# Row transposes of the second to fifth expert: two blocks (three tiles, then two) in place of five groups of four

## The chip, the cores and the metric

The kernel runs on one core of one Trainium2 chip. The metric is the device time of one execution in microseconds (us). Three executions of the kernel before took 602.71, 602.74 and 603.37 us, median 602.74.

## The reference

Two stages. The first is a causal decayed attention without softmax: for 8 batches and 8 heads of 576 positions by 64 dimensions, `scores = q k^T / 8`, multiplied by a decay matrix `gamma_h ** (i - j)` for `i >= j` (zero above the diagonal), times `v`. Its output is rearranged to 4608 rows (tokens) of 512.

The second is a mixture of eight experts with a fixed capacity. `logits = x @ w_gate` (4608 x 8); all 36,864 pairs of token and expert are sorted by logit, and in that order a token goes to the expert if it has none yet and the expert has fewer than 576 tokens. Each expert then has exactly 576 rows, and its output is `relu(x[mask] @ w1[e]) @ w2[e]`, with w1 of 512 x 1024 and w2 of 1024 x 512, written back to the rows' places.

## The kernel before, in words

The attention takes the first quarter of the time. What follows is the routing and the experts, interleaved: while TensorE multiplies for one expert, VectorE finds by a radix search which 576 tokens go to a later expert. The eight experts are handled in the order in which the search fills them; below they are called the first to the eighth (`e` = 0 to 7 in the code).

Every float32 operand is split into a high and a low part (`xh`, `xl`; `w1h`, `w1l`; ...), and a product is three matmuls (high by high, low by high, high by low). For one expert the work runs like this:

- `gather(e)` (line 1061): POOL issues five indirect DMAs (L1072) that bring the 576 rows of the expert into the tile `xg`, 128 rows each, the last one 64. It also sets `state['arrives']`, the planner's time from which the rows are taken to be there.
- `transposes(e)` (line 1127), a generator: for each of the five row tiles j, four TensorE transposes (L1163) of 128 x 128 into one PSUM tile `pt`; then ScalarE copies it to `xh` (L1165), and VectorE makes `xl` (L1166). The five tiles `pt` lie in PSUM under the tags t, h0, h1, h0, h1. The tag t has one buffer, h0 and h1 have two each, taken in turn. The first expert uses the tags t and y instead, and experts from the sixth on are transposed in other ways (lines 1136 and 1129).
- `l1(e, tr)` (line 1172): 16 tiles `ph` (8 blocks of hidden units x 2 parts of the rows, 256 and 320), 12 matmuls each (L1209). Their PSUM buffers are of the same tags h0 (first part) and h1 (second part), but for the third and the sixth pair, which use y. ScalarE writes the high part after the ReLU (L1219), and `low` on VectorE the low part (L1181: one instruction for a 256-row tile, two for a 320-row one). `low` of a tile is issued one tile later; that of the sixteenth and last is kept in `owed` and issued in the next stage.
- `l2(e, hb)` (line 1337): five row tiles t of 8 steps f each (L1357): three matmuls of 512 columns in a step, two for the last row tile. In each step, after the matmuls: `mix.adv` (the planner), `owed` at f = 1 (line 1360), gathers, weight conversions (`conv`, L1000 and L1010 on ScalarE, L1012 on POOL), and then lines 1373 to 1375: when the planner's time has passed `state['arrives']`, the generator of the next expert's transposes is made, and from then on one `next(tr)` is called per step. So each group of four transposes comes behind one step's matmuls.

The order on each engine is fixed when the program is built, by a planner (`Mixer`, line 885). It keeps a time `t` for TensorE (each step adds its estimate, 650 ns in `l2`, 430 for the last row tile) and `v` for VectorE (`mix.vec(610)` for each transposed tile, for example). A step of the search (nine matmuls L357 on TensorE, then about 15 VectorE instructions, L361 to L352) is put in at the first `mix.adv` at which `t` has passed the time that `v` allows; some of them (line 354, third entry) one `adv` later. Engines execute in that order; what is computed from what is guarded by semaphores. `pt` in a buffer that a `ph` held before waits until that tile's ScalarE and VectorE readers are done.

The lines that write, read and hold the buffers: line 1161 takes the PSUM tile of a group, line 1202 that of an `l1` tile:

```
pt = P['bank'](("t", "h0", "h1", "h0", "h1")[j] if e else ("t", "y", "y", "t", "y")[j], [128, 4, 128], "pt", F32R)
ps = P['bank']("y" if i // 2 in (2, 5) else f"h{s}", [128, n], "ph")
```

Of the kernel before, what the change touches and what calls it, by code (L numbers as in the profile page):

```python
# [11 lines left out]
F32 = mybir.dt.float32  # L12
F32R = mybir.dt.float32r
# [3 lines left out]
ALU = mybir.AluOpType  # L17
AF = mybir.ActivationFunctionType
# [921 lines left out]
def moe(tc, nc, P, R, xd, w1_d, w1q_d, w2_d, out, mix):  # L940
    V, A, T = nc.vector, nc.scalar, nc.tensor
# [4 lines left out]
    state = dict(dma=0, conv=0, most=2, listing=-1, force=False, asked=set())  # L946
# [114 lines left out]
    def gather(e, all=False, behind=None):  # L1061
        if e == E or not ready(e):
            return
        if e not in state['asked']:
            state['asked'].add(e)
            if e not in XG:
                XG[e] = P["c"].tile([128, 20, 128], F32, name="xg", tag="xg")
            xg = XG[e]
            if e < QUART:
                for j in range(5):  # L1070
                    n = 128 if j < 4 else 64
                    nc.gpsimd.indirect_dma_start(out=xg[:n, 4*j:4*j+4, :].rearrange("p a c -> p (a c)"), out_offset=None, in_=xd[:, :],  # L1072
                                                 in_offset=bass.IndirectOffsetOnAxis(ap=found[e][:n, j:j+1], axis=0))
                state['arrives'] = mix.t + (11800 if e == 3 else 9000)
            else:
                LEFT[e] = list(range(18))
                state['arrives'], state['next'], state['at'] = 0, 0, {}
        left = LEFT.get(e)
        while left and (all or mix.t >= state['next']):
            g = left.pop(0)  # L1080
            if behind is not None:
                nc.gpsimd.tensor_copy(spacer4, behind.bitcast(F32))
            nc.gpsimd.indirect_dma_start(out=XG[e][:, g, :], out_offset=None, in_=xq,  # L1083
                                         in_offset=bass.IndirectOffsetOnAxis(ap=lines[e][:, g:g+1], axis=0))
            state['next'] = mix.t + 1200
            state['at'][g] = mix.t + (6000 if e >= FAST else 13000)

    def fast_transposes(e):

        xg = XG[e]  # L1090
        x = P['s'].tile([128, 4, 2, 288], F32, name="xt", bufs=1)
        xh, xl = [P['s'].tile([128, 7, 2, 288], F32R, name=n, bufs=1) for n in ("xh", "xl")]
        XH[e], XL[e] = xh, xl
        high = lambda i, q: A.activation(xh[:, i], x[:, q], AF.Copy)
        low = lambda i, q: V.tensor_tensor(xl[:, i], x[:, q], xh[:, i].bitcast(F32), op=ALU.subtract)
        less = lambda to, a, b: V.tensor_tensor(x[:, to], x[:, a], x[:, b], op=ALU.subtract)
        for g0, g1 in ((0, 4), (4, 8), (8, 9), (9, 12), (12, 16), (16, 18)):
            while not state['force'] and state['at'].get(g1 - 1, mix.t + 1) > mix.t:
                yield
            th, c = (0, 32*g0) if g0 < 9 else (1, 32*g0 - 288)  # L1100
            V.transpose(x[:, 2*th:2*th+2, :, c:c+32*(g1-g0)].rearrange("p q d (g i) -> p (q d) g i", i=32),
                        xg[:, g0:g1].rearrange("p g (h i) -> p h g i", h=4))
            if g1 == 9:
                high(0, 0)
                high(1, 1)
            elif g1 == 12:
                low(0, 0)
                low(1, 1)
            yield
        high(2, 3)  # L1110
        less(0, 2, 0)
        less(2, 3, 2)
        yield
        high(6, 2)
        low(2, 3)
        less(3, 3, 0)
        yield
        high(5, 3)
        less(1, 1, 3)
        yield  # L1120
        high(4, 0)
        high(3, 1)
        for i, q in ((6, 2), (5, 3), (4, 0), (3, 1)):
            low(i, q)
        yield

    def transposes(e):

        if e >= FAST:
            yield from fast_transposes(e)  # L1130
            return
        xg = XG[e]
        xh = P['s'].tile([128, 4, 576], F32R, name="xh", bufs=1)
        xl = P['s'].tile([128, 4, 576], F32R, name="xl", bufs=1)
        XH[e], XL[e] = xh, xl
        if e >= QUART:
            xt = P['s'].tile([128, 4, 576], F32, name="xt", bufs=1)
            low = lambda c: V.tensor_tensor(xl[:, :, c], xt[:, :, c], xh[:, :, c].bitcast(F32), op=ALU.subtract)
            last = None
            for j in range(5):  # L1140
                n = 4 if j < 4 else 2
                while not state['force'] and state['at'].get(4*j + n - 1, mix.t + 1) > mix.t:
                    yield
                c = slice(128*j, 128*j + 32*n)
                V.transpose(xt[:, :, c].rearrange("p h (g i) -> p h g i", i=32),
                            xg[:, 4*j:4*j+n].rearrange("p g (h i) -> p h g i", h=4))
                A.activation(xh[:, :, c], xt[:, :, c], AF.Copy)
                if last is not None:
                    low(last)
                    mix.vec(1360)  # L1150
                else:
                    mix.vec(680)
                last = c
                yield
            low(last)
            mix.vec(400)
            yield
            return
        for j in range(5):
            n = 128 if j < 4 else 64  # L1160
            pt = P['bank'](("t", "h0", "h1", "h0", "h1")[j] if e else ("t", "y", "y", "t", "y")[j], [128, 4, 128], "pt", F32R)
            for d in range(4):
                T.transpose(pt[:, d, :n], xg[:n, 4*j + d].bitcast(F32R), P['ident_r'][:n, :n])  # L1163
            o, l = [x[:, :, j*128:j*128+n] for x in (xh, xl)]
            A.activation(o, pt[:, :, :n].bitcast(F32), AF.Copy)  # L1165
            V.tensor_tensor(l, pt[:, :, :n].bitcast(F32), o.bitcast(F32), op=ALU.subtract)  # L1166
            mix.vec(610)
            yield

    owed, behindhand = [], []  # L1170

    def l1(e, tr):
# [12 lines left out]
        for i, (f, s) in enumerate(order):  # L1185
# [22 lines left out]
            for k, (w, x) in enumerate(terms):  # L1208
                T.matmul(ps, w, x, start=(k == 0), stop=(k == 11))  # L1209
                if k % 3 == 2:  # L1210
                    mix.adv(320 + 80*s)
                    if e + 1 < QUART:
                        gather(e + 1)
                if k == 5 and i and e + 1 >= QUART:
                    if i % 4 != 3 or e + 1 == FAST and i > 8:
                        gather(e + 1, behind=last)
                    elif i == 7 and behindhand:
                        behindhand.pop(0)()
# [18 lines left out]
    def l1_fast(e, tr):  # L1237
# [18 lines left out]
        def high(k, q, x):  # L1256
            nonlocal done
            h = place(k, q)
            A.activation(h, x, AF.Relu)
            done += 1  # L1260
            if e + 1 < E and done % 4 != 3:
                gather(e + 1, behind=h[0:1, 0:1])
            elif done == 7 and behindhand:
                behindhand.pop(0)()
# [72 lines left out]
    def l2(e, hb):  # L1337
# [54 lines left out]
        if e + 1 < E:  # L1392
            mix.drain(lambda: ready(e + 1))
            gather(e + 1, True)
            if e + 1 not in XH:
                tr = transposes(e + 1)
# [37 lines left out]
def build(tc, nc, qk, vk, cst, er, wg, rf, w1, w1q, w2, out):  # L1434
    with ExitStack() as top:
# [33 lines left out]
        with ExitStack() as ctx:  # L1469
            Q = dict(P)  # L1470
            for name, bufs in (("a", 1), ("ld", 2), ("w", 2), ("xt", 2)):
                Q[name] = ctx.enter_context(tc.tile_pool(name="a_" + name, bufs=bufs))
            R, rows = attention(tc, nc, Q, qk, vk, cst, er, wg, rf, xd, Lg)

            def idle(what):

                if what in ("row", "rows"):
                    if rows:
                        rows.pop(0)()
                    else:  # L1480
                        warm(1)
                    what = 2*(what == "rows")
                if what:
                    warm(what)
            R.idle = idle
            run = moe(tc, nc, P, R, xd, w1, w1q, w2, out, mix)
            mix.drain(lambda: 0 in run.regs)
            while rows:
                rows.pop(0)()
# [29 lines left out]
```

## Time and profile before

| | |
|---|---|
| median of three runs | 602.74 us (602.71 to 603.37) |
| the profiled execution | 602.33 us, its span 600.4 us |
| PE (TensorE matmul) busy | 586.5 us, 98% of the span |
| PEld (weight load) busy | 500.3 us, 83% |
| DVE (VectorE) busy | 472.2 us, 79% |
| ACT (ScalarE) busy | 297.0 us, 49% |
| POOL (GpSimd) busy | 195.2 us, 33% |

The span is the time between the first and the last instruction of the profiled execution; the 1.9 us beside it are the start and the end of the execution. Busy time of TensorE is modelled, since matmuls overlap, so costs on it are read as differences between start times. In rows of the timeline the columns are start (us), duration of the merged group (us), engine, line and operation, what is written and read, shapes, and a count; in brackets the idle time of the engine before it and what ended that.

### The profile page before, as it was taken

Reading aid. Unit: us, or ns where it says so; the run is one execution under the profiler, and the core shown is the slowest. Engines: PE = TensorE matmul, PEld = TensorE weight load, DVE = VectorE, ACT = ScalarE, POOL = GpSimd, SP = SyncE. Lnnn points to the kernel's source line nnn. Section 1 sums busy time; section 2 is a strip of 40 time slices with the busy share of each in tenths; the row PEclk is TensorE's granted clock in tenths of the full one; section 3 lists DMA queues with packets and bytes.
Section 4 is the critical chain, followed back from the end, with each engine's and each line's share of the span. In section 5 each row is a group of like instructions: output and inputs, shape, how many; then the busy total and the mean of one; then the engine's idle time right before and its main releaser. Section 6 shows DMA issues by size and latency. Waiting matters only on the chain.

```text
span 600.4 us, 14947 instructions
## 1 busy us (share of the span) xinstructions
PE 586.5 (98%) x5664; PEld 500.3 (83%) x5664; DVE 472.2 (79%) x1669; ACT 297.0 (49%) x647; POOL 195.2 (33%) x262
## 2 busy tenths in 40 slices
PE   8999999998999999999999999999999999999995
PEld 5887877785599789878987997799789879988973
DVE  3788989798799888987996897799894687888800
ACT  4555554542354547532662456154627358548610
POOL 0000000000511363351632362257647835761021
PEclk9999999999999999999999999999999999999998
DMA  8999999954568699896899199739877724943410
GB/s 321 402 382 331 394 348 370 345 157 157 175 184 176 194 241 236 224 216 188 172 264 257 46 222 236 236 71 246 206 203 154 209 86 113 275 126 92 111 44 35
DMA packets 52063, 126.79 MB, mean 211 GB/s; under 512 B 6400, under 2 KB 20352, under 8 KB 51992
## 3 DMA queue, kind: packets, MB, share of 16 engines
q1 hardware_dynamic: 36340, 80.82, 39.2%
q0 software_dynamic: 15328, 44.58, 33.0%
q8 instruction: 44, 0.72, 0.5%
q10 hardware_dynamic: 324, 0.45, 0.2%
q14 instruction: 27, 0.22, 0.1%
HBM read 81.26 MB, written 19.92 MB: 169 GB/s over the span
## 4 chain that ended last, share of the span: by engine, by line
PE 84%; issue 6%; DVE 3%; DMA 3%; ACT 1%; POOL 1%; POOLq 0%; SPq 0%; DVEq 0%; ACTq 0%
PE py L1357 31%; PE ph L1209 26%; PE pA L602 6%; PE pX L646 4%; PE ph L1287 4%; PE pS L625 3%; PE pX L637 2%; DMA qin<-in_qk 2%; PE r L357 2%; PE pT L684 1%; PE pt L1163 1%; PE pT L698 1%; PE warm L1457 1%; PE pXt L654 1%; POOL out_y L1331 1%
## 5 line engine op out<-in xcount | busy, mean ns | idle before, releaser
L1357 PE MATMUL py<-w2h,hb 128*128 128x512 f32 x576 | 186.9, 396 | 0.0
L1357 PE MATMUL py<-w2l,hb 128*128 128x512 f32 (+1 forms) x320 | 125.1, 391 | 0.0
L1357 PEld LDWEIGHTS py<-w2h,hb 128*128 128x128 f32 x576 | 104.8, 188 | 22.1
L1209 PE MATMUL ph<-xh,w1h 128*128 128x256 f32 (+1 forms) x384 | 110.6, 302 | 0.2 <-ACT xh L1165 0.2
L1209 PE MATMUL ph<-xh,w1l 128*128 128x256 f32 (+1 forms) x384 | 108.5, 296 | 0.0
L1209 PE MATMUL ph<-xl,w1h 128*128 128x256 f32 (+1 forms) x384 | 108.3, 296 | 0.0
L1219 ACT ACTIVATE hb<-ph 128x256 fp32r<-128x256 f32 (+1 forms) x96 | 39.2, 408 | 74.6 <-PE ph L1209 73.2
L1331 POOL DMA_INDIRECT out_y<-yt,idx x40 | 43.8, 1094 | 95.0 <-ACT yt L1378 74.6
L1209 PEld LDWEIGHTS ph<-xh,w1h 128*128 128x128 f32 x384 | 70.9, 190 | 1.2 <-ACT xh L1165 0.7
L1209 PEld LDWEIGHTS ph<-xl,w1h 128*128 128x128 f32 x384 | 71.2, 190 | 0.2
L1209 PEld LDWEIGHTS ph<-xh,w1l 128*128 128x128 f32 x384 | 71.2, 190 | 0.0
L1357 PEld LDWEIGHTS py<-w2l,hb 128*128 128x128 f32 (+1 forms) x320 | 56.7, 177 | 12.9
L1083 POOL DMA_INDIRECT xg<-xd,quart x54 | 56.2, 1040 | 15.4 <-issue 12.9
L1012 POOL DMA_DIRECT2D w2l<-raw x40 | 36.9, 1109 | 60.8 <-ACT hb L1219 48.9
L586 ACT ACTIVATE vin<-vin,cst 128x128 f32<-128x128 f32 (+1 forms) x160 | 48.2, 379 | 5.4 <-DMA vin<-in_vk 3.0
L1181 DVE SCALAR_TENSOR_TENSOR hb<-ph,hb 128x256 fp32r<-128x256 f32 (+1 forms) x144 | 42.7, 349 | 10.4 <-ACT hb L1219 9.7
L1405 POOL DMA_INDIRECT xg<-xd,it x1 | 1.0, 1045 | 147.6 <-DVE sm L421 147.6
L604 DVE TENSOR_TENSOR am<-pA,cst 128x1024 f32<-128x1024 f32 x32 | 38.9, 1214 | 12.8 <-PE pA L602 12.6
L1378 ACT ACTIVATE yt<-py 128x512 f32<-128x512 f32 x32 | 19.0, 592 | 60.5 <-PE py L1357 51.1
L1287 PE MATMUL ph<-xh,op 128*128 128x288 f32 x224 | 46.5, 299 | 0.2
L602 PEld LDWEIGHTS pA<-qin,kin 64*128 64x128 f32 x512 | 31.5, 189 | 10.8 <-issue 4.7
L627 ACT ACTIVATE S<-pS 128x128 f32<-128x128 f32 x64 | 17.8, 278 | 44.0 <-PE pS L625 43.9
(213 smaller groups left out, 1135.6 us busy)
## 6 DMA issues: line engine op xcount, KB each, us to landing
raw<-in_w SPq DMA_DIRECT2D x52, 512.0 KB, 5.4
w1l<-raw POOLq DMA_DIRECT2D x21, 512.0 KB, 6.7
w2l<-raw POOLq DMA_DIRECT2D x16, 512.0 KB, 5.8
kin<-in_qk SPq DMA_DIRECT2D x14, 576.0 KB, 8.0
qin<-in_qk SPq DMA_DIRECT2D x14, 576.0 KB, 6.7
vin<-in_vk SPq DMA_DIRECT2D x14, 576.0 KB, 8.0
nin<-in_vk SPq DMA_DIRECT2D x14, 512.0 KB, 8.5
xd<-xr SPq DMA_DIRECT2D x36, 192.0 KB, 7.9
```

The source lines that it names most:

```text
L586: nc.scalar.activation(x, x, AF.Copy, scale=vs[:, u % HP, 4*c+h:4*c+h+1])
L602: nc.tensor.matmul(pa[:, r, j], LD[u, 'k'][half(r), s], LD[u, 'q'][half(r), s], start=True, stop=True, skip_group_check=True)
L604: nc.vector.tensor_tensor(AM[u, hf], pa, m1[:, None, None, :].to_broadcast([128, 2, 4, 128]), op=ALU.mult)
L646: nc.tensor.matmul(PX[u, hf][half(h), b, 128*c:128*c+128], v[:, a:a+64], AM[u, hf][:, h ^ b, j], start=False, stop=False, skip_group_check ...
L1012: nc.gpsimd.dma_start(lo[:, c], raw[:, c], accum_op=ALU.add)
L1083: nc.gpsimd.indirect_dma_start(out=XG[e][:, g, :], out_offset=None, in_=xq, in_offset=bass.IndirectOffsetOnAxis(ap=lines[e][:, g:g+1], axi ...
L1181: V.scalar_tensor_tensor(hb[:, f, to+a:to+b], ps[:, a:b], 0.0, hb[:, f, 256*s+a:256*s+b].bitcast(F32), op0=ALU.max, op1=ALU.subtract)
L1209: T.matmul(ps, w, x, start=(k == 0), stop=(k == 11))
L1219: A.activation(hb[:, f, c], ps, AF.Relu)
L1287: T.matmul(ps, a, x, start=(j == 0 and (late or i in (1, 2, 7))), stop=(j == 5), skip_group_check=True)
L1331: st = nc.gpsimd.indirect_dma_start(out=out[:, :], out_offset=bass.IndirectOffsetOnAxis(ap=found[e][:n, t:t+1], axis=0), in_=y[:n], in_off ...
L1357: T.matmul(ps[:m], a, w, start=(k == 0), stop=(k == last), skip_group_check=True)
```

## The change

For the second to fifth expert (`e` = 1 to 4), `transposes` issues the twelve transposes of the tiles 0, 1 and 2 in one go, then their three ScalarE copies and three VectorE subtractions, and after two calls of `next` that do nothing, the eight transposes of the tiles 3 and 4 with their copies and subtractions. The first expert keeps five groups. `state['arrives']` is set 2000 ns (planner's time) later for the experts `e` < 5 that are gathered in this way.

```diff
-                state['arrives'] = mix.t + (11800 if e == 3 else 9000)
+                state['arrives'] = mix.t + (13800 if e == 3 else 11000)
...
-        for j in range(5):
-            n = 128 if j < 4 else 64
-            pt = P['bank'](("t", "h0", "h1", "h0", "h1")[j] if e else ("t", "y", "y", "t", "y")[j], [128, 4, 128], "pt", F32R)
-            for d in range(4):
-                T.transpose(pt[:, d, :n], xg[:n, 4*j + d].bitcast(F32R), P['ident_r'][:n, :n])
-            o, l = [x[:, :, j*128:j*128+n] for x in (xh, xl)]
-            A.activation(o, pt[:, :, :n].bitcast(F32), AF.Copy)
-            V.tensor_tensor(l, pt[:, :, :n].bitcast(F32), o.bitcast(F32), op=ALU.subtract)
-            mix.vec(610)
+        for js in ((0, 1, 2), (3, 4)) if e else ((0,), (1,), (2,), (3,), (4,)):
+            pts = []
+            for j in js:
+                n = 128 if j < 4 else 64
+                pt = P['bank'](("t", "h0", "h1", "h0", "h1")[j] if e else ("t", "y", "y", "t", "y")[j], [128, 4, 128], "pt", F32R)
+                pts.append((j, n, pt))
+                for d in range(4):
+                    T.transpose(pt[:, d, :n], xg[:n, 4*j + d].bitcast(F32R), P['ident_r'][:n, :n])
+            for j, n, pt in pts:
+                o, l = [x[:, :, j*128:j*128+n] for x in (xh, xl)]
+                A.activation(o, pt[:, :, :n].bitcast(F32), AF.Copy)
+                V.tensor_tensor(l, pt[:, :, :n].bitcast(F32), o.bitcast(F32), op=ALU.subtract)
+                mix.vec(610)
             yield
+            if len(js) == 3:
+                yield
+                yield
```

## Rows read from the trace of the kernel before

**Rows 1.** Windows: busy us (instructions) of PE, PEld, DVE, ACT, POOL, clock, DMA, GB/s.
```profile
219.00:556.00 337.00, 336.83 (x2315) 298.57 (x2314) 276.82 (x1056) 176.47 (x321) 163.08 (x218) 1.00 0.73 187
```

**Rows 2.** Waits of PE and PEld: who for whom, us in total, times, longest us.
```profile
PE ph L1209 <- ACT xh L1165: 0.2, 1, 0.2
...
PEld pt L1163 <- DVE hb L1181: 0.3, 1, 0.3
```

**Rows 3.** Timeline of PE, fifth expert's transposes.
```profile
359.89 0.39 PE L357 MATMUL r<-oh,G 128*128 128x32 bf16 x9
360.13 0.70 PE L1357 MATMUL py<-w2h,hb 128*128 128x512 f32 x2
360.67 0.39 PE L1357 MATMUL py<-w2l,hb 128*128 128x512 f32 x1
360.90 0.46 PE L1163 MATMUL pt<-ident,xg 128*128 128x128 f32 x4
361.19 0.70 PE L1357 MATMUL py<-w2h,hb 128*128 128x512 f32 x2
...
361.95 0.46 PE L1163 MATMUL pt<-ident,xg 128*128 128x128 f32 x4
...
364.08 0.53 PE L1163 MATMUL pt<-ident,xg 128*128 128x128 f32 x4
...
364.97 0.40 PE L1357 MATMUL py<-w2l,hb 128*128 128x512 f32 x1
365.21 0.39 PE L357 MATMUL r<-oh,G 128*128 128x32 bf16 x9
365.53 0.50 PE L1163 MATMUL pt<-ident,xg 64*128 64x64 f32 x4
365.96 0.72 PE L1357 MATMUL py<-w2h,hb 128*128 128x512 f32 x2
...
366.75 0.61 PE L1357 MATMUL py<-w2h,hb 128*128 128x512 f32 x2
...
367.43 0.61 PE L1357 MATMUL py<-w2h,hb 128*128 128x512 f32 x2
```

**Rows 4.** Timeline of PE, first expert: eight transposes in a row.
```profile
161.76 0.80 PE L1163 MATMUL pt<-ident,xg 128*128 128x128 f32 x8
```

**Rows 5.** Timeline of PE, third expert: last tile without a search step ahead of it.
```profile
262.56 0.40 PE L1357 MATMUL py<-w2l,hb 128*128 128x512 f32 x1
262.88 0.49 PE L1163 MATMUL pt<-ident,xg 64*128 64x64 f32 x4
263.31 0.73 PE L1357 MATMUL py<-w2h,hb 128*128 128x512 f32 x2
...
264.11 0.62 PE L1357 MATMUL py<-w2h,hb 128*128 128x512 f32 x2
```

**Rows 6.** Timeline of DVE, same place as rows 3.
```profile
359.63 0.88 DVE L1181 SCALAR_TENSOR_TENSOR hb<-ph,hb 128x256 fp32r<-128x256 f32 x3
360.43 0.14 DVE L361 SCALAR_TENSOR_TENSOR cs<-room,r 32x8 f32<-32x8 f32 x1
...
363.59 0.42 DVE L1181 SCALAR_TENSOR_TENSOR hb<-ph,hb 128x256 fp32r<-128x256 f32 x1
363.93 0.68 DVE L1166 TENSOR_TENSOR xl<-pt,xh 128x512 fp32r<-128x512 f32 x1
364.53 0.54 DVE L1181 SCALAR_TENSOR_TENSOR hb<-ph,hb 128x256 fp32r<-128x256 f32 x2
364.99 1.87 DVE L1166 TENSOR_TENSOR xl<-pt,xh 128x512 fp32r<-128x512 f32 x3
```

**Rows 7.** Timeline of ACT, same place as rows 3.
```profile
362.31 1.80 ACT L1165 ACTIVATE xh<-pt 128x512 fp32r<-128x512 f32 x3
```

**Rows 8.** Timeline of POOL: last gather of the fifth expert's rows.
```profile
349.96 1.30 POOL L1072 DMA_INDIRECT xg<-xd,idx  x1 [0.30 <-issue]
```

## The prediction

> **What bounds the kernel now.** I read three kinds of view in this order: busy time by stage, the list of waits of TensorE, then the timelines around the transposes of the four experts that the change touches. In the stage that holds most of the change, from 219 to 556 us, TensorE is busy 336.83 of 337.00 us at a granted clock of 1.00 [rows 1]. Its waits in the whole run are few and short: for an `xh` it waited 0.2 us once, and at the transposes of the experts concerned there is one wait for VectorE, 0.3 us of the weight queue's time [rows 2]. So the end is set by how many TensorE starts stand in line and how far apart they are. ScalarE, VectorE and POOL matter only where they make TensorE wait. What the change takes off TensorE is gained in full, and any wait that it puts there is paid in full, because nothing later is waiting for anything else.
>
> **The change part by part.** *Fewer interruptions.* A step of three matmuls alone takes 0.68 us (start 366.75 to 367.43) [rows 3]. From the start of a group of four to the start of the next group are 1.05 us (360.90 to 361.95), so the group costs 0.37: 0.29 for the transposes themselves, 0.08 by which the step behind it is longer [rows 3]. In a longer row the transposes are not as cheap as the first four: eight in a row are 0.80 us, less the 0.25 of the last one's own length 0.55 between the first and the eighth start; 0.30 of that goes to the first four, leaving 0.084 for each further one [rows 4]. The block of twelve therefore costs 0.30 + 8 x 0.084 + 0.08 = 1.05, against 3 x 0.37 = 1.11 to 1.14. I take 0.08 saved.
>
> The last tile (64 rows) costs 0.09 of extra gap ahead (262.56 to 262.88 where 0.23 is usual), 0.43 for the transposes and 0.12 in the step behind (0.80 for 0.68), 0.64 in all [rows 5]. In the second block the fourth tile stands directly ahead of it and its own 0.08 exit goes: 0.94 against 1.01. Together 0.16 per expert, 0.64 us over four.
>
> Against this: a group directly behind a search step shares the step's exit. In the fifth expert the last tile stands so: 0.32 + 0.43 + 0.11 = 0.86 with the search step, where the two apart would be 0.24 + 0.09 + 0.64 = 0.97 [rows 3, 5]. Each of the four experts has one such neighbourhood now, about 0.3 us together (0.11 twice, about half that for an ordinary tile). With two blocks in place of five groups I count two left, 0.1. Gain: 0.64 - 0.2 = 0.44 us (bounds: 0.2 if no neighbourhood is left, 0.96 if all twelve exits of 0.08 go without the dearer starts).
>
> The Trainium skill (TensorE: Matmul & The Clock Gate, "Wait — 56ns, not 53.3ns?") gives about 56 ns from start to start for warm matmuls of 128 columns. By it the transposes behind the first four would cost less than the 84 ns of the rows, and the gain over four experts would be an estimated 1.3 us, 8 x 0.028 more for each of four blocks; the row of eight does not bear that out, and I do not use it.
>
> *Later start.* 2000 planner ns are three steps. For the second, third and fourth expert each tile is transposed later than its rows needed before, so no gather is newly waited for, and the planned end stays at least five steps ahead of the first layer. VectorE and ScalarE do the same work, bunched; their cover is the rest of `l2`. For these experts I cost it at nothing. For the fifth expert the 2000 ns do not bind: its last gather is issued at 349.96 [rows 8], and the first `l2` step ends at 360.90 with the group at once behind it [rows 3]. So its first block stays at the first step, f = 0.
>
> *The wait that is added, and it is in the fifth expert.* The tiles 3 and 4 take the second buffers of h0 and h1, which the fifteenth and the sixteenth `ph` of `l1` held just before. That this is live shows already: the one wait for `hb` is the fourth group at 364.08 [rows 2, 3], right after VectorE's single `low` instruction of 363.59 [rows 6]. The sixteenth `ph` is released by the owed `low`, two instructions at 364.53 [rows 6]. It is issued at f = 1. Before, only one `xl` stands ahead of it (363.93); after, the first block is issued whole at f = 0, so three `xl` stand ahead of it, and the second block, at f = 3, has tile 4 waiting for it. Queued behind the waiting transposes is all of TensorE.
>
> Which VectorE work stands ahead of that `low` depends also on where the planner puts the sixth expert's third search step, L357 at 359.89, whose VectorE part runs from 360.43 to 363.59, 3.16 us [rows 3, 6]. I carried the planner's sums by hand from the second expert on, from its constants (610 a tile, 650 a step, the search steps' own estimates). A block bills its three tiles together after a search step where single groups were partly billed in idle planner time, so `v` comes out a few hundred ns later each time. For that search step the sum gives one place later: behind the first `l2` step, directly ahead of the first block. Then:
> - TensorE: the first step starts at 359.89, the search step at 360.58, the block at 360.82; 0.34 + 8 x 0.084 = 1.01 to 361.83; three steps 0.76 + 0.68 + 0.68 to 363.95; tile 3 to 364.25; tile 4 wants to start at 364.35.
> - VectorE: its part of the search step starts 0.43 behind L357 (0.54 in rows 3 and 6, where other work stood ahead), at 361.01, ends at 364.17; three `xl` at 0.60 each (363.93 to 364.53) to 365.97; the owed `low`, 0.54, to 366.51. The `xh` that they need are ready by then: three copies from 362.31 take 1.80 [rows 7].
> - TensorE waits from 364.35 to about 366.55, 2.2 us.
>
> Sum: -0.44 + 2.2 = +1.75; with the small wait of the fourth group gone, +1.7 us. On the profiled execution, 602.33, that is 604.0; it lay 0.41 under the median of the runs, so the time forecast is 602.74 + 1.7 = 604.4.
>
> **The rivals.** (1) *The search step keeps its place* ahead of `l2`. Then VectorE is free at 363.59: 0.34 for the fifteenth `low`, 1.80 for three `xl`, 0.5 for the owed `low`, to 366.25; tile 4 wants 364.40. Wait 1.85, net +1.4: 604.1. For it: several passes in the planner's sum are decided by 5 to 30 of its ns.
> (2) *It slips two places*, into f = 1 ahead of the owed `low`: three `xl` to 364.7, 3.16 of search to 367.9, the `low` to 368.4, tile 4 wants 364.7. Wait 3.7, net +3.2: 606.0.
> (3) *It slips three or more.* Then only the three `xl` are ahead, bounded by ScalarE: first `xh` done at 362.9, `xl` to 364.7, `low` to 365.2. Wait 0.8, net +0.4: 603.1, within what a measurement can tell from no change.
> (4) *The gain alone, faster than before.* Were the owed `low` ahead of the block's `xl`, or the buffers taken in another turn, nothing would be added: -0.45, 602.3. Against it is the wait that the rows show on just these buffers [rows 2].
> (5) *Everything better than the rows*: no wait, no neighbourhood lost (0.2 more), and the further transposes at the first four's pace, 0.29 / 4 = 0.073 (4 x 8 x 0.011 = 0.35 more): -1.0, 601.7, which a lucky run puts past what can be told. The row of eight speaks against it [rows 4].
> Forecast, (1) and (2) are slower, (4) and (5) are the other side; the point that decides is whether tile 4's first transpose of the fifth expert starts later than 364.4.
>
> A stall of this length might also lower the granted clock, which is 1.00 throughout the stage [rows 1]; no row shows such a stall there, and I cost it at nothing.
>
> **How the numbers follow.** 0.2% of the time, 1.2 us, is about what a measurement of this kernel can tell from no change. Chances: the forecast 0.50 (of it 0.42 above the bound, since a 0.5 us smaller wait falls inside), rival (1) 0.10, half above, (2) 0.12, all above, (3) 0.13, (4) 0.11, (5) 0.04, counted as faster than the bound; (3) and (4) are the same. Slower 0.42 + 0.05 + 0.12 = 0.59, faster 0.04, same 0.37. The likeliest alone: 603.9 to 604.9. The range to 8 in 10 reaches from just above the gain alone to rival (2): 602.5 to 606.1.
>
> **What would show it.** In the timeline of TensorE the second to fifth expert have `pt` x12 and then x4 and x4, with the step behind each block at 0.76 to 0.80; the twelve take about 0.97 us. In the list of waits, `pt` waits for `hb` of VectorE about 2 us, once, in the fifth expert. In VectorE's timeline three `xl` in a row stand ahead of two L1181 instructions there. The forecast is wrong if that wait is missing or under 1 us, if the block of twelve is much shorter than 0.97, or if another expert's transposes wait.

## The result

The changed kernel takes 609.49 us (median of 4 runs, 606.61 to 610.87), the kernel before 603.0; the ratio is 1.0101, interval 1.0063 to 1.0139. So it is slower, as forecast, but by 6.5 us where 1.7 were forecast, and outside the range. Its profiled execution took 608.95 us (span 607.0), against 602.33 (600.4). Of the four runs of before, three are those shown ahead. Three later sets of runs, on three chips and with both kernels side by side, give less: 1.0067 (1.0045 to 1.0089), 1.008 (1.006 to 1.0099) and 1.0067 (1.0046 to 1.0088), some 4.1 to 4.8 us; that is what the change costs on these chips.

The windows of the kernel after (columns as in [rows 1]), the whole stretch first:
```profile
219.00:562.00 343.00, 338.23 (x2311) 299.36 (x2310) 277.58 (x1055) 175.11 (x319) 160.63 (x218) 1.00 0.72 183
...
368.00:370.00 2.00, 2.00 (x9) 1.59 (x10) 1.25 (x4) 1.59 (x3) 0.00 (x0) 0.76 0.95 234
370.00:372.00 2.00, 2.00 (x14) 1.38 (x13) 0.94 (x6) 0.68 (x1) 0.89 (x2) 0.50 0.39 123
```
In [rows 1] TensorE idled 0.17 us; here it idles 4.77, and in one stretch its clock is at half: 1.2 GHz for 2.4. Its waits (who for whom, us in total, times, longest):
```profile
PE pt L1166 <- DVE xl L1170: 1.8, 1, 1.8
PE r L357 <- DVE G L181: 1.7, 2, 1.1
...
PE py L1364 <- issue: 1.2, 2, 0.8
```
None of these three is in the list of waits of the kernel before. Each has its place. (`issue` stands where the profile shows nothing that the engine waited for.) First, TensorE at the fifth expert's transposes, which stand in the fourth expert's second layer, to be laid beside [rows 3]:
```profile
362.01 0.39 PE L1364 MATMUL py<-w2l,hb 128*128 128x512 f32 x1
362.24 0.39 PE L357 MATMUL r<-oh,G 128*128 128x32 bf16 x9
362.48 1.18 PE L1166 MATMUL pt<-ident,xg 128*128 128x128 f32 x12
363.50 0.70 PE L1364 MATMUL py<-w2h,hb 128*128 128x512 f32 x2
...
365.64 0.46 PE L1166 MATMUL pt<-ident,xg 128*128 128x128 f32 x4
367.87 0.50 PE L1166 MATMUL pt<-ident,xg 64*128 64x64 f32 x4 [1.77 <-DVE xl L1170]
```
The search step stands directly ahead of the block, as worked out, and tile 4 waits: it could start about 366.04 (365.64 + 0.30 for tile 3 + 0.1) and starts at 367.87, 1.83 us late. VectorE there, beside [rows 6]:
```profile
362.77 0.14 DVE L361 SCALAR_TENSOR_TENSOR cs<-room,r 32x8 f32<-32x8 f32 x1
...
365.93 1.89 DVE L1170 TENSOR_TENSOR xl<-pt,xh 128x512 fp32r<-128x512 f32 x3
367.73 0.54 DVE L1188 SCALAR_TENSOR_TENSOR hb<-ph,hb 128x256 fp32r<-128x256 f32 x2
```
The search part takes 3.16 us (362.77 to 365.93) as before, then come three `xl`, then the owed `low`. But tile 4 starts as the third `xl` ends (367.82), while the `low` is still running. So it has not got the sixteenth `ph`'s buffer; it stands on that of tile 2.

Second, two search steps on TensorE, in the second expert's second layer and in the fourth expert's first layer:
```profile
259.88 0.39 PE L1364 MATMUL py<-w2l,hb 128*128 128x512 f32 x1
261.37 0.39 PE L357 MATMUL r<-oh,G 128*128 128x32 bf16 x9 [1.10 <-DVE G L181]
...
356.71 0.31 PE L1216 MATMUL ph<-xh,w1l 128*128 128x320 f32 x1
357.59 0.39 PE L357 MATMUL r<-oh,G 128*128 128x32 bf16 x9 [0.57 <-DVE G L181]
```
The starts are 1.49 and 0.88 us apart where 0.23 and 0.15 is usual: 1.26 and 0.73 lost. Ahead of the first, VectorE itself began late:
```profile
257.05 0.20 DVE L352 TENSOR_TENSOR u<-v,D 128x36 f32<-128x36 bf16 x1
258.28 0.15 DVE L361 SCALAR_TENSOR_TENSOR cs<-room,r 32x8 f32<-32x8 f32 x1 [1.04 <-PE py L1364]
```
L361 reads what TensorE's L357 at 256.36 wrote, 0.39 us of work, and starts 1.9 us behind its start. Ahead of the second, VectorE is not idle: five `low` instructions, 1.34 us from 353.20, stand ahead of its L361 at 354.46. Third, in the sixth expert's second layer, ScalarE's copy of the first row tile, whose matmuls began at 474.87 and take some 5.6 us ("remote": the profile knows a release but not its sender):
```profile
479.64 1.32 ACT L1044 ACTIVATE op<-raw 128x256 fp32r<-128x256 f32 x4
486.06 0.60 ACT L1385 ACTIVATE yt<-py 128x512 f32<-128x512 f32 x1 [5.11 <-remote]
```
TensorE then pauses twice in the second row tile. By the starts of the stages in both timelines, the layer takes 27.02 us, 1.53 more than before. All stages (the layers of the experts) together: 1.07 for the two that the first search step delays, 0.62 for the other's, 3.02 for the one with the fifth expert's transposes, 0.47 in the two stages after, 1.53 here, less small differences elsewhere: the 6.6 us between the profiles. Parts of the search also stand in another stage than before, so the shares of single stages hold moved work too.

### The profile page after: what moved, and what is told of

It reads as the page before. It is cut to its first block, busy times and chain, and to the rows that moved or that the text cites. A ratio compares the mean times of both kernels' runs of the same rounds, so it can differ in the third digit from the quotient of the medians.

```text
span 607.0 us, 14944 instructions
## 1 busy us (share of the span) xinstructions
PE 589.2 (97%) x5664; PEld 502.2 (83%) x5664; DVE 472.8 (78%) x1669; ACT 295.9 (49%) x647; POOL 193.5 (32%) x262
## 4 chain that ended last, share of the span: by engine, by line
PE 79%; DVE 10%; issue 6%; ACT 1%; POOL 1%; DMA 1%; POOLq 0%; DVEq 0%; ACTq 0%
PE py L1364 29%; PE ph L1216 22%; PE pA L602 6%; PE pX L646 4%; PE ph L1294 4%; PE pS L625 3%; PE pX L637 2%; PE pT L684 2%; PE r L357 1%; DVE hb L1188 1%; PE pt L1166 1%; DVE G L181 1%; PE pT L698 1%; PE warm L1464 1%; DVE f L365 1%
## 5 line engine op out<-in xcount | busy, mean ns | idle before, releaser
L1364 PEld LDWEIGHTS py<-w2h,hb 128*128 128x128 f32 x576 | 106.2, 189 | 24.0 <-issue 1.0
```

The lines of the kernel that those rows point to most:

```text
L1364: T.matmul(ps[:m], a, w, start=(k == 0), stop=(k == last), skip_group_check=True)
```

## The experiments

In what follows, theory A and the rivals are those of the expectations that stand ahead of each run. There are four sets; the kernels of one set ran on one chip, beside runs of the kernel before, whose medians were 603.76, 602.01, 604.72 and 604.20. The changed kernel comes again in three of them.

**Set 1: one part at a time.** *The owed `low` first*, ahead of the block's `xl`; by the program's buffer assignment tile 4 then gets the other buffer:
```
+            if e and owed:
+                owed.pop()()
             for j, n, pt in pts:
```


> The changed kernel, but the owed low of the fifth expert is issued ahead of the three xl of its first block. The buffers then come free in another order: tile 4 gets the one of the sixteenth ph instead of the one of tile 2. Theory A (the wait and the fall of the clock behind it are made by tile 4's buffer): the wait of 1.8 us at tile 4 shrinks to about 0.5 us or none (the low ends near 366.5, tile 4 wants to start near 366.0), the granted clock stays 1.00 from 366 to 374, and the kernel is 2.9 to 3.4 us faster than the changed one: 605.5 to 606.6. Theory B (the clock falls there for another reason, such as bunched work of the other engines): the wait goes but the clock still falls, gain 1.3 to 1.8 us: 607.7 to 608.2.

605.22 us, ratio 1.0021 (1.0007 to 1.0035); 2.6 us faster than the changed kernel beside it, a little less than the 2.9 to 3.4 expected. TensorE, then VectorE:
```profile
364.99 0.46 PE L1166 MATMUL pt<-ident,xg 128*128 128x128 f32 x4
365.91 0.47 PE L1166 MATMUL pt<-ident,xg 64*128 64x64 f32 x4 [0.47 <-issue]
```
```profile
365.26 0.56 DVE L1190 SCALAR_TENSOR_TENSOR hb<-ph,hb 128x256 fp32r<-128x256 f32 x2
365.73 2.47 DVE L1172 TENSOR_TENSOR xl<-pt,xh 128x512 fp32r<-128x512 f32 x4
```
The wait is 0.47; the profile names no releaser, but the `low` ends just ahead of it (365.82). The clock is 1.00 from 366 to 374. Theory A, on both counts: with the blocks as they are, the order of these VectorE instructions decides over most of the wait, and without the long wait the clock does not fall.

*The later start alone*, on the kernel before:
```
-                state['arrives'] = mix.t + (11800 if e == 3 else 9000)
+                state['arrives'] = mix.t + (13800 if e == 3 else 11000)
```


> The kernel before, five groups of four, with only the later start (11000 and 13800). The search steps then stand where they stand in the changed kernel. Theory A (the later start moves the search steps, and two of them then wait for VectorE): L357 waits near 260 and near 357 as in the changed kernel, together about 2.0 us, no wait at tile 4, clock 1.00: 604.5 to 605.5. Rival (it is the bunched xl and xh of the blocks that make VectorE late for the search step): no such wait, 602.5 to 603.4. The stall of 1.5 us in the sixth expert's second layer, if it comes from the search steps' places, shows here too (606 to 607).

606.31 us, ratio 1.0045 (1.003 to 1.0061), above what was expected. Both waits of L357 are there (1.10 at 260.91, 0.56 at 357.78), so they come from the later start, through the places of the search steps, and need no block. Beyond them there is a wait of 0.51 for `xl` at 218.32, at the first matmul of the second expert's first layer (here the later start does make a tile late), and the loss in the sixth expert.

*The blocks alone*, with the old start:
```
-                state['arrives'] = mix.t + (13800 if e == 3 else 11000)
+                state['arrives'] = mix.t + (11800 if e == 3 else 9000)
```


> The changed kernel with the old start (9000 and 11800): blocks alone. Theory A: the search steps stand as before or nearly so, so the two waits of L357 are gone (2.0 us); in the fifth expert the third search step stands behind the last transposes, so only three xl are ahead of tile 4's buffer: a wait of about 0.8 us or less, and with so short a wait the clock stays at 1.00. 603.0 less 0.4 plus 0.8: 602.6 to 604.0. Rival (the blocks themselves cost it): 607 to 609.5.

606.72 us, ratio 1.0045 (1.0032 to 1.0058): a miss. Neither of the two waits of L357 is there, but others in the fifth expert's second layer, and the wait at tile 4 is longer than the 0.8 expected:
```profile
363.15 0.54 PE L1166 MATMUL pt<-ident,xg 128*128 128x128 f32 x4
364.94 0.50 PE L1166 MATMUL pt<-ident,xg 64*128 64x64 f32 x4 [1.26 <-DVE xl L1170]
```
Its clock is 0.50 from 366 to 368. The search step kept its place (L357 at 358.97, ahead of the layer): the mechanism of the prediction's rival 1, with tile 2's `xl` as the releaser.

*The changed kernel again.*

> The changed kernel once more, to see which of its waits come back. Theory A: the wait of about 1.8 us at tile 4 of the fifth expert and the two waits of L357 (1.3 and 0.7 us) are in every execution, since they follow from the order of the instructions; the median is 608.5 to 610.5. The stall of 1.5 us near 485 and the depth and length of the clock's fall may differ. Rival: the waits are chance events of one execution, and this profile has others.

607.83 us, ratio 1.0067, somewhat under the 608.5 to 610.5 expected. All waits named above come back, the first search step with 1.09, tile 4 with 1.76, and the fall of the clock.

**Set 2: what is the change's at all.** *The kernel before, again.*

> The kernel before, profiled once more beside the variants, to see whether two losses that all five profiles of variants show are the change's at all: about 1.2 to 1.5 us in the sixth expert's second layer (ScalarE's first yt stands 4 to 5 us idle, TensorE's last py of the second row tile pause), and about 1.0 us by which VectorE's part of the search step near 257 starts late. Theory A (they belong to the conditions of these executions and not to the change): this profile shows both, and its time is 603.5 to 605. Theory B (they come from the later order of the instructions): neither shows, the time is 602.4 to 603.8.

602.31 us. Neither loss shows (ScalarE's `yt` stands without idle at 476.77). Nor does either show in the next two, changed, kernels on this chip, though both show in all of set 1.

*Blocks, old start, owed `low` first* (both edits of set 1 together).

> The changed kernel with the old start (9000 and 11800) and with the owed low of the fifth expert ahead of its xl: blocks alone, without the wait at tile 4 and without the moved search steps. Theory A (the blocks themselves gain 0.44 us, as predicted; all the rest is the wait, the clock and the places of the search steps): no wait of TensorE over 0.3 us at the transposes, clock 1.00, ratio to the kernel before 0.998 to 1.001. Rival (blocks cost something by themselves, such as VectorE's bunched work making search steps late): ratio 1.002 to 1.004.

601.27 us, ratio 0.9991 (0.9976 to 1.0006): the forecast gain of 0.44 us is 0.9993, and this agrees with it, but the interval takes in no change, so no gain is shown. There is no wait at tile 4. There is one for the gather, of the fourth expert's rows, since its block now wants them early:
```profile
308.25 1.08 PE L1166 MATMUL pt<-ident,xg 128*128 128x128 f32 x8 [0.31 <-DMA xg<-xd,idx]
```

*The fifth expert in five groups*, the rest as changed:
```
-        for js in ((0, 1, 2), (3, 4)) if e else ...
+        for js in ((0, 1, 2), (3, 4)) if 0 < e < 4 else ...
```


> The changed kernel with the fifth expert in five groups of four again. Tile 4 then gets the sixteenth ph's buffer, as before the change. Theory A (wait and clock are both the fifth expert's second block): no wait over 0.5 us at its transposes, clock 1.00, and a time like that of the kernel with the owed low first: ratio to the kernel before 1.001 to 1.004, against 1.005 to 1.009 of the changed kernel. Rival (a block elsewhere costs): ratio above 1.005.

602.64 us, ratio 1.002 (1.0009 to 1.0031), as theory A has it; clock 0.998. The search steps and the last tile on TensorE:
```profile
259.02 0.39 PE L357 MATMUL r<-oh,G 128*128 128x32 bf16 x9
...
355.33 0.39 PE L357 MATMUL r<-oh,G 128*128 128x32 bf16 x9 [0.52 <-DVE G L181]
...
364.92 0.47 PE L1166 MATMUL pt<-ident,xg 64*128 64x64 f32 x4 [0.25 <-issue]
```
In this version the second to fourth expert keep their blocks. The first search step no longer waits, though it stands in the same place of the order: here VectorE's L361 was on time (255.94, right behind L352 at 255.69). So that 1.1 us needs both, the step's place and VectorE's late start; the 0.5 at 355 needs the place alone (VectorE's five `low` ahead of L361 stand here too).

*Four stalls put by hand into the kernel before*, in the second layers of the second to fifth expert:
```
+                if t == 2 and f == 3 and e in (1, 2, 3, 4):
+                    pz = P['bank']("t", [128, 128], "pz")
+                    T.matmul(pz, P['z'][:, :128], P['z'][:, :128], start=True, stop=True)
+                    for _ in range((1, 2, 3, 5)[e - 1]):
+                        nc.gpsimd.memset(P['z'], 0.0)
+                    T.matmul(pz, P['z'][:, :128], P['z'][:, :128], start=True, stop=True)
```


> The kernel before with four stalls of TensorE put in by hand, in the fourth step of the third row tile of the second to the fifth expert's second layer: a matmul of 128 columns, then 1, 2, 3 and 5 memsets on GpSimd that wait for it, then another such matmul that waits for them. Its own time means nothing; it shows from what stall on the granted clock falls behind py matmuls, and what that costs beyond the stall. Theory A (a stall of about 1.3 us or more lowers the clock to 0.50 for some 3 us, wherever it stands): the longer two or three lower it, the shortest doesn't. Rival (it needs the block of transposes ahead of the stall): none of them lowers it below 0.9 in a stretch of 1 us.

The run took 618.57 us, and the stalls came out as 0.65, 1.91, 2.38 and 8.08 us, on TensorE; then windows behind the second and the third, and one that begins inside the fourth:
```profile
262.12 0.23 PE L1365 MATMUL pz<-z 128*128 128x128 bf16 x1 [0.65 <-POOL z L1364]
...
321.62 0.23 PE L1365 MATMUL pz<-z 128*128 128x128 bf16 x1 [1.91 <-POOL spacer L1330]
...
382.79 0.23 PE L1365 MATMUL pz<-z 128*128 128x128 bf16 x1 [2.38 <-POOL spacer L1330]
...
445.79 0.29 PE L1365 MATMUL pz<-z 128*128 128x128 bf16 x1 [8.08 <-POOL spacer L1330]
```
```profile
323.00:326.00 3.00, 3.00 (x9) 2.36 (x8) 0.00 (x0) 0.03 (x1) 0.00 (x0) 0.51 0.90 236
384.00:387.00 3.00, 3.00 (x23) 2.31 (x22) 1.35 (x8) 0.60 (x1) 0.00 (x0) 1.00 1.03 279
443.00:449.00 6.00, 3.21 (x9) 2.53 (x10) 0.00 (x0) 0.00 (x0) 2.53 (x6) 0.50 0.98 242
```
Neither theory as it stood: no transposes are needed, but length does not decide either. 1.91 us lowered the clock, 2.38 did not. Beside the kernel before on this chip, the stages with the 0.65 and the 2.38 us are 0.3 to 0.5 us longer than their stalls; with the 1.91 and the 8.08 us it is 1.9 and 2.0, so by an estimate a fall cost 1.4 to 1.7 us. The Trainium skill (TensorE: Matmul & The Clock Gate, "What's actually happening") has the gate look at stretches that run freely, not from a kernel's own events; by that the same stall can lower it or not. These rows fit that; no run here shows what the gate looks at.

**Set 3.** *Before, after, the later start alone, and blocks with old start and owed `low` first*, on one more chip.

> The kernel before once more, as a profile beside the three that follow on the same chip. In the two sets so far the losses near 257 and in the sixth expert's second layer showed in every profile of one set and in none of the other, whatever the kernel. Theory A (they go with the chip or its conditions): this profile shows them if the three others do, and not if they don't. Theory B (they go with the kernel): it never shows them.

> The changed kernel, timed five rounds. What the kernel itself must lose by the steps found so far: wait at tile 4 about 1.8 us in every execution, the search step in the fourth expert's first layer 0.7 us, the clock's fall 0 or about 1.6 us by chance, less 0.44 us gain. Theory A: where the other losses don't show, ratio 1.003 to 1.007 (2 to 4 us over before); where they do, 1.006 to 1.010. Rival (the losses of the first profiles are all the change's): 1.008 to 1.011 on any chip.

> Only the later start, five groups of four, on this chip. Theory A: the one wait of L357 in the fourth expert's first layer, 0.7 us, and no more: ratio 1.0005 to 1.002 where the two other losses don't show, 1.004 where they do. Rival (the later start alone costs some 2.5 us anywhere): 1.004.

> The blocks with the old start and the owed low first, once more, to narrow the interval and to see the gain on another chip. Theory A (gain 0.44 us, no new wait): ratio 0.998 to 1.0005. Rival (nothing gained): 1.000 to 1.002.

The kernel before shows the sixth expert's loss itself:
```profile
479.91 0.60 ACT L1378 ACTIVATE yt<-py 128x512 f32<-128x512 f32 x1 [5.02 <-remote]
```
Its layer takes 28.16 us there (468.53, worked out, since the first matmul is missing from the records, to 496.69), 2.67 over the profile shown ahead. VectorE starts late near 257 in it too:
```profile
255.58 0.19 DVE L352 TENSOR_TENSOR u<-v,D 128x36 f32<-128x36 bf16 x1
256.55 0.15 DVE L361 SCALAR_TENSOR_TENSOR cs<-room,r 32x8 f32<-32x8 f32 x1 [0.78 <-PE r L357]
```
The L357 that this reads is at 254.94, 1.61 us earlier; in the profile shown ahead L361 starts at once when VectorE is free. After: 609.54, ratio 1.008 (1.006 to 1.0099), tile 4 waits 1.76, the clock falls. The later start alone: 607.75, 1.005 (1.0031 to 1.0069). The fourth, which set 2 had at 0.9991, is 1.0026 (1.0013 to 1.0039) here, a miss. In it VectorE starts late twice:
```profile
256.78 0.15 DVE L361 SCALAR_TENSOR_TENSOR cs<-room,r 32x8 f32<-32x8 f32 x1 [1.16 <-PE py L1366]
...
418.19 0.15 DVE L361 SCALAR_TENSOR_TENSOR cs<-room,r 32x8 f32<-32x8 f32 x1 [1.93 <-remote]
```
At 256.78 that costs TensorE nothing (the next L357 is at 259.87, without a wait); behind 418.19 its L357 waits 0.94 at 420.96. The wait for the gather is 0.80. So no version here is shown to be faster than the kernel before.

**Set 4.** *Before, after, owed `low` first, later start alone*, on a fourth chip.

> The kernel before as a profile beside the three that follow on the same chip, to see which of the two conditions holds here: the loss in the sixth expert's second layer (ScalarE's first yt some 5 us idle) shows in the kernel before, or it doesn't.

> The changed kernel on one more chip. Theory A (its own loss is the wait at tile 4, 1.8 us, the clock's fall behind it by chance, 0 to 1.6, and the search step of the fourth expert's first layer, 0.7, less a gain of 0.44; the search step near 261 costs 1.1 more only where TensorE's signal near 257 is late): without late signals ratio 1.0035 to 1.006 and no wait of L357 near 261; with them 1.006 to 1.010. Rival (1.008 or more, on any chip).

> The changed kernel with the owed low ahead of the block's xl, on this chip. Theory A: 1.8 us of wait less, and the clock's fall gone: 2 to 3.5 us faster than the changed kernel beside it, whatever the condition of the chip; without late signals ratio to before 1.000 to 1.0025. Rival: the difference to the changed kernel is under 1.5 us.

> Only the later start. Theory A: without late signals 0.7 us from the search step of the fourth expert's first layer, ratio 1.000 to 1.002; with them 1.004 to 1.006 as in the two sets before. Rival: 1.004 or more in both conditions.

The kernel before again has the sixth expert's loss (27.22 us) and the late start near 257 (0.66 us idle ahead of L361 at 256.60), and also one long wait of a search step:
```profile
419.86 0.39 PE L357 MATMUL r<-oh,G 128*128 128x32 bf16 x9 [1.41 <-DVE G L181]
```
After: 608.44, ratio 1.0067 (1.0046 to 1.0088). Owed `low` first: 605.97, 1.0025 (1.001 to 1.004), 2.5 us less than after, as in set 1. Later start alone: 606.5, 1.0039 (1.0025 to 1.0053). This profile of after has tile 4's wait without the fall:
```profile
367.78 0.50 PE L1166 MATMUL pt<-ident,xg 64*128 64x64 f32 x4 [1.75 <-DVE xl L1170]
```
```profile
368.00:370.00 2.00, 2.00 (x20) 1.53 (x19) 1.16 (x4) 1.68 (x3) 0.00 (x0) 1.00 1.02 272
```
The stage with the fifth expert's transposes takes 31.09 us in it (361.48 to 392.57) against 32.67 in the first profile of after (361.54 to 394.21): the fall costs 1.58 us. A mean clock of 0.995 or less over a run, taken as the sign of a fall, stands in 15 of 22 runs of after, in 0 of 24 with the owed `low` first, and in 7 of the 95 of before (5 of them among the 17 of set 3; no profile shows why).

## Why the prediction was wrong

The forecast was one wait of 2.2 us less a gain of 0.44. The wait came. What failed are two terms that were put at nothing: the fall of the clock behind the wait, and the later start.

**The gain was right piece by piece, a little high; no run shows it in the time.** The fourth expert's blocks in the kernel after, beside [rows 3 to 5]:
```profile
310.80 1.15 PE L1166 MATMUL pt<-ident,xg 128*128 128x128 f32 x12
311.79 0.70 PE L1364 MATMUL py<-w2h,hb 128*128 128x512 f32 x2
...
312.55 0.63 PE L1364 MATMUL py<-w2h,hb 128*128 128x512 f32 x2
...
313.93 0.89 PE L1166 MATMUL pt<-ident,xg 128*128 128x128 f32 x8
314.75 0.73 PE L1364 MATMUL py<-w2h,hb 128*128 128x512 f32 x2
...
315.56 0.39 PE L357 MATMUL r<-oh,G 128*128 128x32 bf16 x9
```
Twelve transposes 0.99 and a step of 0.76 behind them, 1.07 with its 0.08 (forecast 1.05); the second block 0.82 and a step of 0.81, 0.95 (forecast 0.94). Each further transpose is (0.99 - 0.30) / 8 = 0.086 us, where 0.084 was forecast. The Trainium skill (TensorE: Matmul & The Clock Gate, "Wait — 56ns, not 53.3ns?") gives 0.056 for such matmuls back to back; the trace doesn't agree here either.

**The wait of the fifth expert was right in place and nearly in size.** 1.83 for 2.2, the search step where the sum put it, tile 4 the one that waits. Its releaser was not the owed `low` but the third `xl`: that tile 4 takes the sixteenth `ph`'s buffer was wrong, and so was the description ahead that the two buffers of a tag are taken in turn. Tile 2's `xl` is issued ahead of the owed `low`, and in both orders that were run tile 4 had the buffer whose release is issued first; with the `low` issued first it had the other one. The owed `low` would have made it 2.2 (it ends at 368.27), so that the forecast came near in size is in part luck: the tile waited for another instruction. Rival 4 named the cure: with the `low` ahead, 0.47 is left.

**"I cost it at nothing" of the clock failed.** The paragraph saw that a stall of this length might lower it, and took 0 for a term that is 0 or 1.58 us, and which falls in 15 of 22 runs: 1.1 in the mean. The sum had only the lower of its two values, and the range lacked it.

**"For these experts I cost it at nothing" of the later start failed.** The step looked for tiles that would be late, and in the changed kernel there are none. What moved were the search steps of other experts, which the planner fits in by its running sum; the forecast followed that sum only to the one place ahead of the fifth expert's block. Two others now stand where VectorE has not finished: one idles TensorE 0.52 to 0.61 us in every profile with the later start (0.73 from start to start), the other 1.09 to 1.21 in those in which VectorE also starts late near 257. In the kernel before, on two chips, VectorE starts late there as well (0.78 and 0.66 us), and TensorE does not wait: the step's old place left room for it. The later start alone measured 2.3 to 3.0 us, with waits of its own.

Sum: -0.4 + 1.83 (tile 4) + 1.1 (clock, in the mean) + 0.73 + 1.1 (search steps) = 4.4, for 4.1 to 4.8 measured side by side. This is an estimate from single waits: it leaves out some 0.5 us in the two stages behind tile 4, which a later start alone shows too, and what the sixth expert's layer differs between the profiles. The rest of the first 6.5 is the sixth expert's layer: 1.53 in that profile of after, none in the profile of before. As the kernel before has the same loss on two of the chips, it does not take the change to bring it. What makes it, and VectorE's late start, is open: in both an engine that waits for TensorE starts 0.7 to 5 us later than it could by the records of the work that it waits for, and no run took it apart. Both losses show in every profile of sets 1, 3 and 4 (in 3 and 4 the kernel before included) and in none of set 2, so they go with the chip or its condition. Near 257 the late start is smaller in the kernel before (0.66 and 0.78) than in the variants (1.00 to 1.16), so the order of instructions may have a part in its size. Neither the changed kernel nor the later start alone was run on the chip of set 2, where neither loss shows.

## What to carry to other kernels

When an edit changes a number that a planner adds up, list every item that the planner places afterwards, on every engine, not only the items edited. Where a block needs several buffers, read from the program's assignment which buffer each tile gets, since issuing a release earlier can be worth more than the block: 2.5 us here, against a forecast 0.4. And a stall of the lengths that lowered the clock here (1.26 us was the shortest) is priced at itself and at itself plus 1.6, both in the range.

## What was not expected of the hardware

The granted clock fell from 1.00 to 0.50 behind stalls of 1.26 (blocks alone), 1.77 (after) and 1.91 us (by hand) and within the one of 8.08 (by hand), and stayed at 1.00 behind 1.41 (before, set 4), 1.75 (after, set 4) and 2.38 (by hand). The fall is worth 1.58 us by the two profiles of the same kernel, nearly as much as the wait that brings it. The same program differs between chips by more than the change that was forecast: medians of before of 602.01 to 604.72, with one layer of 25.5 us taking 27.2 and 28.2.
